# Retention plus two feed-forward layers: the second batch's state products on the other two array quadrants

## The chip, the cores and the metric

The kernel runs on one core of a Trainium2 chip. Its time is the device time of one execution in microseconds (us); given are the median of three runs and one execution that the hardware profiler recorded. The engines: TensorE (PE, with its weight loads as PEld), VectorE (DVE), ScalarE (ACT), GpSimd (POOL) and SyncE (SP), which here issues all DMAs.

## What is computed

Retention over 2 batches, 8 heads, 768 positions and head size 64, and then two feed-forward layers, all in float32:

```python
for t in range(S):
    state = gamma * state + einsum('bhd,bhe->bhde', k[:, :, t], v[:, :, t])
    y[:, :, t] = scale * einsum('bhd,bhde->bhe', q[:, :, t], state)
x = y.transpose(0, 2, 1, 3).reshape(B * S, H * D)      # 1536 x 512
h = x @ w1_in;  x = softplus(h) @ w1_out               # 512 -> 2048 -> 512
h = x @ w2_in;  out = silu(h) @ w2_out
```

## The kernel before

**Retention in chunks.** The 768 positions of each batch are cut into 6 chunks of 128, so there are 12 chunks, numbered n with the batch as n % 2: chunks 2 and 3 are the same positions of the two batches. Heads are taken in four pairs. For a chunk, `att_scores` (line 161) multiplies keys and queries of a head (64 rows of the array), `att_mask` (line 172) puts on the decay on DVE, and `att_within` (line 180) multiplies the result by the values: 128 rows, 64 columns, the even head j = 0 of a pair into PSUM partitions 0 to 63 and the odd head j = 1 into 64 to 127 of the tile `py`. `att_across` (line 196) adds what earlier chunks left: queries scaled by GpSimd (`qp`, line 125) times the state `past`, 64 rows and 64 columns of the array per head. Head j reads SBUF partitions of half j and writes PSUM partitions of half j, so of the four 64x64 quadrants only the two on the diagonal work. `att_state` (line 143) adds the chunk's keys (`kp`, scaled by GpSimd, line 132) times values to the state in PSUM, and `att_past` (line 158) copies that to SBUF on ACT.

**The split.** The feed-forward products run as three matmuls of a rounded high part and a low part. `att_split` (line 210) makes these of a chunk's output: `xhi` on ACT from `py` (line 219), `xlo` = `py` - `xhi` on DVE (line 220). Four chunks make a block of 512 tokens. `gemm1(i, half)` (line 316) reads `xhi` and `xlo` of a whole block: steps 0 to 2 read chunks 0 to 3, steps 3 to 5 chunks 4 to 7, steps 6 to 8 chunks 8 to 11. Step 0 alone goes by halves of 256 tokens, chunks 0 and 1 first.

**Weights.** They arrive as 64-bit numbers. A unit of them is converted by one ACT copy (`z`, line 267), six DVE instructions (lines 274, 275, 284, 287, 290, 292) and one ACT copy (`whi`, line 303).

**Order.** The order of each engine's work is the order of the program text, written out by hand (lines 452 to 576): chunk pair 2 and 3 stands in the main text (lines 497 to 519); pairs 4, 6, 8 and 10 go through `att_pair` (line 222), each behind a `gemm1` of 12 matmuls and the conversion of a weight unit. After pair 10 the rest is feed-forward steps alone.

Of the kernel before, what the change touches and what calls it, by code (L numbers as in the profile page):

```python
# [9 lines left out]
F32 = mybir.dt.float32  # L10
# [4 lines left out]
AF = mybir.ActivationFunctionType  # L15
# [3 lines left out]
P = 128  # L19
B, H, S, D = 2, 8, 768, 64  # L20
NCH = S // P
NPAIR = H // 2
DM = H * D
# [52 lines left out]
def retention_ffn2_kernel(  # L76
# [9 lines left out]
    nc = tc.nc  # L86
    const = ctx.enter_context(tc.tile_pool(name="const", bufs=1))
# [12 lines left out]

    mask = const.tile([P, 2, NPAIR, P], F32, name="mask")
    cs = const.tile([P, H * NCH], F32, name="cs")
    zero = const.tile([P, DM], F32, name="zero")

# [2 lines left out]
    a_t, qs_t, qp_t, kp_t, ps_t, sc_t, py_t, x_t = {}, {}, {}, {}, {}, {}, {}, {}  # L109
    state = ps.tile([P, B, NPAIR, D], F32, tag="st", bufs=1, name="state")  # L110
    past = const.tile([P, B, NPAIR, D], F32, name="past")
# [13 lines left out]
    def att_scale_q(n):  # L125
        qp = apool.tile([P, NPAIR, P], F32, tag="qp", name=f"qp{n}")
        qp_t[n] = qp
        nc.gpsimd.tensor_tensor(
            out=qp.rearrange("p a t -> p (a t)"), in0=a_t[n][:, 0, :], in1=qs_t[n // B], op=ALU.mult
        )  # L130
# [12 lines left out]
    def att_state(n):  # L143
        b, c = n % B, n // B
        a, kp = a_t[n], kp_t.pop(n)
        for p in range(NPAIR):
            for j in range(2):
                h = 2 * p + j
                nc.tensor.matmul(  # L149
                    state[j * D : (j + 1) * D, b, p, :],  # L150
                    lhsT=kp[:, h, :],
                    rhs=a[:, 2, h * D : (h + 1) * D],
                    start=n == p == 0,
                    stop=c == NCH - 2,
                    skip_group_check=True,
                )

    def att_past():
        nc.scalar.activation(out=past, in_=state, func=AF.Copy)

    def att_scores(n):
        a = a_t[n]
        pj = [
            psa.tile([P, NPAIR, P], F32, tag=f"acc{2 * (n % 2) + j}", name=f"sc{n}_{j}") for j in range(2)
        ]
        for p in range(NPAIR):
            for j in range(2):
                r, s = slice(j * D, (j + 1) * D), slice(p * P, (p + 1) * P)
                nc.tensor.matmul(pj[j][:, p, :], lhsT=a[r, 1, s], rhs=a[r, 0, s], start=True, stop=True)  # L169
        ps_t[n] = pj  # L170
# [9 lines left out]
    def att_within(n):  # L180
        a, sc = a_t[n], sc_t.pop(n)
        py = ps.tile([P, NPAIR, P], F32, tag="py", name=f"py{n}")
        py_t[n] = py
        for p in range(NPAIR):
            for j in range(2):
                h = 2 * p + j
                nc.tensor.matmul(  # L187
                    py[j * D : (j + 1) * D, p, :],
                    lhsT=a[:, 2, h * D : (h + 1) * D],
                    rhs=sc[j][:, p, :],  # L190
                    start=(p == 0),
                    stop=(n < B and p == NPAIR - 1),
                    skip_group_check=True,
                )

    def att_across(n):
        py, qp = py_t[n], qp_t.pop(n)
        for p in range(NPAIR):
            for j in range(2):
                r = slice(j * D, (j + 1) * D)  # L200
                nc.tensor.matmul(  # L201
                    py[r, p, :],
                    lhsT=past[r, n % B, p, :],
                    rhs=qp[r, p, :],
                    start=False,
                    stop=(p == NPAIR - 1),
                    skip_group_check=True,
                )

    def att_split(n):  # L210
        py = py_t.pop(n)
        blk, o = n // CPB, (n % CPB) * P
        if o == 0:
            x_t[0, blk] = (
                xpool.tile([P, NPAIR, BLK], F32R, tag="xhi", name=f"xhi{blk}"),
                xpool.tile([P, NPAIR, BLK], F32R, tag="xlo", name=f"xlo{blk}"),
            )
        hi, lo = (t[:, :, o : o + P] for t in x_t[0, blk])
        nc.scalar.activation(out=hi, in_=py, func=AF.Copy)
        nc.vector.tensor_tensor(out=lo, in0=py, in1=hi.bitcast(F32), op=ALU.subtract)  # L220

    def att_pair(n):

        more = n + B < NC
        for b in range(B):
            att_within(n + b)
        for b in range(B):
            att_across(n + b)
            att_split(n + b)
        if more:  # L230
            for b in range(B):
                att_scale_q(n + B + b)
            for b in range(B):
                att_scores(n + B + b)
            for b in range(B):
                att_state(n + b)
            att_past()
            for b in range(B):
                att_mask(n + B + b)
            if n + B < NC - B:  # L240
                for b in range(B):
                    att_scale_k(n + B + b)
# [209 lines left out]
    with tc.manual_schedule():  # L452
        att_load(0, 0, 2)
        nc.sync.dma_start(out=mask, in_=mask_d)
        att_load(1, 0, 2)
        att_load(0, 2, 3)
        att_load(1, 2, 3)
        nc.sync.dma_start(out=cs, in_=cs_d)
        att_load(0, 3, 4)
        att_load(1, 3, 4)  # L460
        att_load(2, 0, 2)
        att_load(3, 0, 2)
        qs_load(1)
        w_load(0)
        att_load(2, 2, 3)
        att_load(3, 2, 3)
        w_load(1)
        att_load(2, 3, 4)
        att_load(3, 3, 4)
        att_load(4, 0, 2)  # L470
        nc.scalar.preload_act_table_set("softplus")
        nc.vector.memset(zero, 0.0)
        warm = ps.tile([P, BLK], F32, tag="h", bufs=1, name="warm")
        for _ in range(WARM):
            nc.tensor.matmul(warm, lhsT=zero[:, :P], rhs=zero, start=True, stop=True)

        att_scores(0)
        att_mask(0)
        att_scores(1)
        att_mask(1)  # L480
        att_within(0)
        att_split(0)
        att_within(1)
        att_split(1)
        att_scale_k(0)
        att_scale_k(1)
        att_state(0)
        att_state(1)
        att_past()
        att_load(5, 0, 2)  # L490
        att_load(4, 2, 3)
        att_load(5, 2, 3)
        qs_load(2)
        w_load(2)
        att_load(4, 3, 4)
        att_load(5, 3, 4)
        att_scores(2)
        att_mask(2)
        att_scores(3)
        att_mask(3)  # L500
        att_scale_q(2)
        att_scale_q(3)
        w_exponent(0)
        convert(0)
        att_within(2)
        att_within(3)
        w_exponent(1)
        att_across(2)
        att_split(2)
        att_across(3)  # L510
        att_split(3)
        gemm1(0, 0)
        gemm1(0, 1)
        att_scale_k(2)
        att_scale_k(3)
        att_state(2)
        att_state(3)
        convert(1)
        act1(0)
        att_past()  # L520
        for lo in (0, 2):
            att_load(6, lo, lo + 2)
            att_load(7, lo, lo + 2)
        w_load(3)
        att_scale_q(4)
        att_scale_q(5)
        att_scores(4)
        att_mask(4)
        att_scores(5)
        att_mask(5)  # L530
        att_load(8)
        qs_load(3)
        att_scale_k(4)
        att_scale_k(5)
        first(1)
        act2(0)
        w_exponent(2)
        convert(2)
        act2(1)
        att_pair(4)  # L540
        att_load(9)
        qs_load(4)
        att_load(10, 0, 3)
        for i, n in ((2, 6), (3, 8), (4, 10)):
            u = units[i][0]
            w_exponent(u)
            first(i)
            convert(u)
            if i < NLEAD - 1:
                act2(i)  # L550
            att_pair(n)
            if n == 6:
                qs_load(5)
                att_load(11, 0, 3)
        second(0)
        act2(4)
        first(5)
        for u in units[5]:
            w_exponent(u)
            convert(u)  # L560
        second(1)
        act2(5)
        second(2)
        first(6)
        for u in units.get(6, ()):
            w_exponent(u)
            convert(u)
        second(3)
        act2(6)
        second(4)  # L570
        for i in range(NLEAD + 2, N):
            step(i)
        for m in range(4):
            gemm2(N - 2, (m,))
            gemm2(N - 1, (m,))
            evacuate(N - 1, (m,))
# [60 lines left out]
```

## Time and profile before

| what | us |
|---|---|
| median of 3 runs (578.09 to 579.44) | 578.32 |
| the profiled execution | 577.85 |
| its span, first to last instruction | 575.9 |
| PE busy in the span | 568.8 |
| DVE busy | 370.1 |
| ACT busy | 197.9 |
| POOL busy | 43.4 |

The profiled execution took 577.85 us, of which 575.9 us lie between its first and its last instruction; it is 0.47 us below the median. Retention and the first steps of the feed-forward lie in the first 64 us or so. In the chain of work that ended last PE has 96% of the span, but this is a figure of the whole span; what the change touches lies in the first eighth.

### The profile page before, as it was taken

The numbers are of one execution on the slowest core, as the hardware profiler recorded it, in microseconds if no ns is written. First come the engines' busy times: TensorE is split into PE (matmuls) and PEld (weight loads), VectorE is DVE, ScalarE is ACT, GpSimd is POOL, SyncE is SP. The second block draws the span as 40 slices with busy tenths as digits, with TensorE's granted clock in tenths as the row PEclk, the third lists the DMA queues.
The fourth block names the chain that finished last, engine by engine and source line by source line (L and its number), as shares of the span: only waits on it lengthen the run. The fifth ranks groups of instructions, "written<-read, shape, count | busy, mean of one in ns | idle before, by whom it ended". The sixth has DMA issues, their size and how long they took to land.

```text
span 575.9 us, 7532 instructions
## 1 busy us (share of the span) xinstructions
PE 568.8 (99%) x3026; PEld 470.2 (82%) x3026; DVE 370.1 (64%) x613; ACT 197.9 (34%) x363; POOL 43.4 (8%) x36
## 2 busy tenths in 40 slices
PE   8999999999999999999999999999999999999997
PEld 5888888888888888888888888888888888888885
DVE  3999458566854865785769863675566764783232
ACT  2343244423423423334336434343234233242120
POOL 1547000000000000000222210000000000000000
PEclk9999999999999999999999999999999999999999
DMA  8994122221211321221213211222113212100111
GB/s 298 399 410 159 36 75 78 69 73 38 99 48 36 110 73 38 73 77 70 74 36 110 74 49 61 73 73 75 36 40 107 74 36 74 49 25 0 74 73 74
DMA packets 15730, 51.10 MB, mean 89 GB/s; under 512 B 1872, under 2 KB 1872, under 8 KB 15440
## 3 DMA queue, kind: packets, MB, share of 16 engines
q1 hardware_dynamic: 15696, 50.63, 25.2%
q8 instruction: 24, 0.39, 0.3%
q14 instruction: 10, 0.08, 0.0%
HBM read 47.47 MB, written 3.15 MB: 88 GB/s over the span
## 4 chain that ended last, share of the span: by engine, by line
PE 96%; DMA 1%; DVE 1%; SPq 1%; POOL 0%; ACT 0%; issue 0%; DVEq 0%; POOLq 0%
PE acc L370 45%; PE h L331 45%; PE sc L169 2%; PE py L201 1%; PE py L187 1%; DMA att<-in_att 1%; PE state L149 1%; POOL kp L136 0%; SPq L123 0%; DVE scm L177 0%; DVE xlo L220 0%; DVE a L287 0%; DVE m L275 0%; DVE part L385 0%; ACT whi L303 0%
## 5 line engine op out<-in xcount | busy, mean ns | idle before, releaser
L347 ACT ACTIVATE ghi<-h 128x512 fp32r<-128x512 f32 x96 | 57.4, 598 | 334.0 <-PE h L331 322.7
L354 DVE TENSOR_TENSOR glo<-t,ghi 128x512 fp32r<-128x512 f32 x96 | 68.1, 714 | 40.4 <-ACT t L348 40.4
L385 DVE TENSOR_TENSOR part<-acc,part 128x512 f32<-128x512 f32 x84 | 57.4, 692 | 50.0 <-PE acc L370 50.0
L331 PE MATMUL h<-xhi,wlo 128*128 128x512 f32 (+1 forms) x196 | 76.0, 388 | 0.0
L331 PE MATMUL h<-xlo,whi 128*128 128x512 f32 (+1 forms) x196 | 75.6, 386 | 0.1
L331 PE MATMUL h<-xhi,whi 128*128 128x512 f32 (+1 forms) x196 | 75.4, 385 | 0.0
L370 PE MATMUL acc<-ghi,wlo 128*128 128x512 f32 x192 | 74.8, 390 | 0.0
L370 PE MATMUL acc<-ghi,whi 128*128 128x512 f32 x192 | 74.7, 389 | 0.0
L370 PE MATMUL acc<-glo,whi 128*128 128x512 f32 x192 | 74.7, 389 | 0.0
L331 PE MATMUL h<-yhi,wlo 128*128 128x512 f32 x192 | 74.7, 389 | 0.0
L331 PE MATMUL h<-ylo,whi 128*128 128x512 f32 x192 | 74.7, 389 | 0.0
L331 PE MATMUL h<-yhi,whi 128*128 128x512 f32 x192 | 74.7, 389 | 0.0
L370 PE MATMUL acc<-whi,glo 128*128 128x512 f32 x192 | 74.7, 389 | 0.0
L370 PE MATMUL acc<-wlo,ghi 128*128 128x512 f32 x192 | 74.7, 389 | 0.0
L370 PE MATMUL acc<-whi,ghi 128*128 128x512 f32 x192 | 74.7, 389 | 0.0
L284 DVE TENSOR_SCALAR z<-z 128x512 uint32<-128x512 uint32 x64 | 28.2, 441 | 71.2 <-ACT z L267 71.2
L348 ACT ACTIVATE t<-h 128x512 f32<-128x512 f32 x96 | 56.9, 593 | 0.0
L287 DVE SCALAR_TENSOR_TENSOR a<-raw,z 128x512 uint32<-128x512 uint32 x64 | 46.2, 722 | 2.2
L275 DVE SCALAR_TENSOR_TENSOR m<-raw,m 128x512 uint32<-128x512 uint32 x64 | 45.4, 710 | 2.2
L292 DVE SCALAR_TENSOR_TENSOR wlo<-m,z 128x512 fp32r<-128x512 int32 x64 | 45.0, 704 | 2.2
L303 ACT ACTIVATE whi<-a 128x512 fp32r<-128x512 f32 x64 | 40.5, 633 | 11.8 <-DVE a L287 11.8
L267 ACT ACTIVATE z<-raw 128x512 f32<-128x512 f32 x64 | 42.7, 668 | 1.6 <-DMA raw<-in_wts 1.6
(41 smaller groups left out, 682.7 us busy)
## 6 DMA issues: line engine op xcount, KB each, us to landing
raw<-in_wts SPq DMA_DIRECT2D x64, 512.0 KB, 3.3
att<-in_att SPq DMA_DIRECT2D x10, 512.0 KB, 7.4
att<-in_att SPq DMA_DIRECT2D x12, 256.0 KB, 7.1
out<-part SPq DMA_DIRECT2D x12, 256.0 KB, 2.1
att<-in_att SPq DMA_DIRECT2D x2, 1024.0 KB, 8.6
att<-in_att SPq DMA_DIRECT2D x2, 768.0 KB, 6.2
qs<-in_qs SPq DMA_DIRECT2D x5, 256.0 KB, 6.8
mask<-in_mask SPq DMA_DIRECT2D x1, 512.0 KB, 5.4
```

The costliest lines, as they stand in the source:

```text
L267: nc.scalar.activation(out=z, in_=raw_t[u][:, :, 1].bitcast(F32), func=AF.Copy, scale=2.0**-112)
L275: nc.vector.scalar_tensor_tensor(out=m, in0=raw[:, :, 1], scalar=23, in1=m, op0=ALU.logical_shift_left, op1=ALU.bitwise_or)
L284: nc.vector.tensor_scalar(out=z, in0=z, scalar1=3, scalar2=4, op0=ALU.logical_shift_left, op1=ALU.bitwise_or)
L287: nc.vector.scalar_tensor_tensor(out=a, in0=raw[:, :, 1], scalar=0x80000000, in1=z, op0=ALU.bitwise_and, op1=ALU.bitwise_or)
L292: nc.vector.scalar_tensor_tensor(out=lo, in0=m.bitcast(I32), scalar=2.0**-43, in1=z.bitcast(F32), op0=ALU.mult, op1=ALU.mult)
L303: nc.scalar.activation(out=hi, in_=a, func=AF.Copy)
L331: nc.tensor.matmul(ph[:, t], lhsT=w[:, s], rhs=x[:, kc, t], start=kc == o == j == 0, stop=kc == NPAIR - 1 and j == 2, skip_group_check=i == 0,
L347: nc.scalar.activation(out=ghi, in_=ph, func=f)
L348: nc.scalar.activation(out=t, in_=ph, func=f)
L354: nc.vector.tensor_tensor(out=glo, in0=t, in1=ghi.bitcast(F32), op=ALU.subtract)
L370: nc.tensor.matmul(acc_t[m], lhsT=lhsT, rhs=rhs, start=(first and j == 0), stop=(last and j == 2))
L385: nc.vector.tensor_tensor(out=part[:, m, :], in0=acc_t[m], in1=part[:, m, :], op=ALU.add)
```

## The change

Chunks of the second batch (odd n) keep the heads of a pair in exchanged halves of the PSUM tile: `half(n, j)` gives partitions of half j for even n and of the other half for odd n. `att_across` takes both chunks of a pair at once and goes through pair of heads, batch, head, so that four matmuls in a row are on the four 64x64 quadrants. `att_split` of an odd chunk first copies the two halves of `py` crosswise into an SBUF tile `turned` (two ACT instructions of 64 partitions by 512), and then makes `xhi` and `xlo` from `turned`. To make room, the tile of zeros for the first three matmuls is gone; `past` is set to zero and read in its place.

```diff
-    zero = const.tile([P, DM], F32, name="zero")
+    turned = const.tile([P, NPAIR, P], F32, name="turned")
@@ att_within
-                    py[j * D : (j + 1) * D, p, :],
+                    py[half(n, j), p, :],
+    def half(n, j):
+        j ^= n % B
+        return slice(j * D, (j + 1) * D)
+
     def att_across(n):
-        py, qp = py_t[n], qp_t.pop(n)
+        qp = [qp_t.pop(n + b) for b in range(B)]
         for p in range(NPAIR):
-            for j in range(2):
-                r = slice(j * D, (j + 1) * D)
-                nc.tensor.matmul(
-                    py[r, p, :],
-                    lhsT=past[r, n % B, p, :],
-                    rhs=qp[r, p, :],
+            for b in range(B):
+                for j in range(2):
+                    r = slice(j * D, (j + 1) * D)
+                    nc.tensor.matmul(
+                        py_t[n + b][half(n + b, j), p, :],
+                        lhsT=past[r, b, p, :],
+                        rhs=qp[b][r, p, :],
@@ att_split
+        if n % B:
+            for j in range(2):
+                nc.scalar.activation(out=turned[half(0, j)], in_=py[half(1, j)], func=AF.Copy)
+            py = turned
         nc.scalar.activation(out=hi, in_=py, func=AF.Copy)
         nc.vector.tensor_tensor(out=lo, in0=py, in1=hi.bitcast(F32), op=ALU.subtract)
@@ att_pair
+        att_across(n)
         for b in range(B):
-            att_across(n + b)
             att_split(n + b)
@@ main text
-        nc.vector.memset(zero, 0.0)
+        nc.vector.memset(past, 0.0)
+        zero = past.rearrange("r b p e -> r (b p e)")
...
         att_across(2)
         att_split(2)
-        att_across(3)
         att_split(3)
```

## Rows read from the trace of the kernel before

**Rows 1.** The page: span, and busy time of each engine with its share.
```profile
span 575.9 us, 7532 instructions
PE 568.8 (99%) x3026; PEld 470.2 (82%) x3026; DVE 370.1 (64%) x613; ACT 197.9 (34%) x363; POOL 43.4 (8%) x36
```
**Rows 2.** By stretch: us, busy us (PE, PEld, DVE, ACT, POOL), clock, DMA share, GB/s.
```profile
32.00:40.00 8.00, 8.00 (x114) 6.87 (x112) 7.83 (x15) 3.12 (x6) 0.74 (x1) 1.00 1.03 409
...
64.00:72.00 8.00, 8.00 (x37) 6.62 (x36) 2.91 (x5) 2.90 (x6) 0.00 (x0) 1.00 0.00 0
```
**Rows 3.** The chain that ended last, to 72 us: start, us, engine and line.
```profile
21.49 0.69 DVE xlo L220
...
22.22 1.57 PE h L331 x11
...
31.70 1.89 PE py L201 x32
...
35.58 1.08 PE state L149 x32
```
**Rows 4.** Timeline, TensorE: start, us, engine, line, operation, out<-in, count, [idle before <-releaser].
```profile
33.52 2.06 PE L169 MATMUL sc<-att 64*128 64x128 f32 x32
...
39.54 1.97 PE L187 MATMUL py<-scm,att 128*64 128x128 f32 x32
...
42.47 0.85 PEld L201 LDWEIGHTS py<-qp,past 64*64 64x64 f32 x16 [0.18 <-POOL qp L128]
...
46.84 0.19 PEld L331 LDWEIGHTS h<-xlo,whi 128*128 128x128 f32 x1
```
**Rows 5.** Timeline, ACT: the splits of chunks 1 to 5 and a copy of the state.
```profile
11.54 0.60 ACT L219 ACTIVATE xhi<-py 128x512 fp32r<-128x512 f32 x1 [0.69 <-PE py L187]
13.43 0.60 ACT L159 ACTIVATE past<-state 128x512 f32<-128x512 f32 x1 [1.29 <-PE state L149]
...
20.26 1.08 ACT L219 ACTIVATE xhi<-py 128x512 fp32r<-128x512 f32 x2
...
33.40 1.07 ACT L219 ACTIVATE xhi<-py 128x512 fp32r<-128x512 f32 x2
```
**Rows 6.** Timeline, DVE: masks of chunk 2, chunk 4's split to chunk 7's, line 287 later.
```profile
14.50 2.48 DVE L177 TENSOR_TENSOR scm<-sc,mask 128x512 f32<-128x512 f32 x4 [1.64 <-PE sc L169]
...
34.53 1.28 DVE L220 TENSOR_TENSOR xlo<-py,xhi 128x512 fp32r<-128x512 f32 x2
...
38.12 0.41 DVE L274 TENSOR_SCALAR m<-raw 128x512 uint32<-128x512 uint32 x1
...
39.18 0.42 DVE L284 TENSOR_SCALAR z<-z 128x512 uint32<-128x512 uint32 x1
39.63 1.65 DVE L287 SCALAR_TENSOR_TENSOR a<-raw,z 128x512 uint32<-128x512 uint32 x1
41.31 1.38 DVE L290 TENSOR_SCALAR z<-a 128x512 uint32<-128x512 uint32 x1
42.73 1.41 DVE L292 SCALAR_TENSOR_TENSOR wlo<-m,z 128x512 fp32r<-128x512 int32 x1
44.07 1.53 DVE L354 TENSOR_TENSOR glo<-t,ghi 128x512 fp32r<-128x512 f32 x1
45.52 1.27 DVE L220 TENSOR_TENSOR xlo<-py,xhi 128x512 fp32r<-128x512 f32 x2
...
59.97 0.69 DVE L287 SCALAR_TENSOR_TENSOR a<-raw,z 128x512 uint32<-128x512 uint32 x1
60.70 0.43 DVE L290 TENSOR_SCALAR z<-a 128x512 uint32<-128x512 uint32 x1
```
**Rows 7.** Timeline, POOL, from 39 us.
```profile
39.26 3.16 POOL L128 TENSOR_TENSOR qp<-att,qs 128x512 f32<-128x512 f32 x2 [8.50 <-DMA qs<-in_qs]
42.37 2.68 POOL L136 TENSOR_TENSOR kp<-att,cs 128x512 f32<-128x512 f32 x2
45.01 2.99 POOL L128 TENSOR_TENSOR qp<-att,qs 128x512 f32<-128x512 f32 x2
```

More of the change, by code (lines that the diff above doesn't have):

```diff
@@ L194, in att_within @@
                 )
+    def half(n, j):
+        j ^= n % B
+        return slice(j * D, (j + 1) * D)
     def att_across(n):
-        py, qp = py_t[n], qp_t.pop(n)
+        qp = [qp_t.pop(n + b) for b in range(B)]
         for p in range(NPAIR):
-            for j in range(2):
-                r = slice(j * D, (j + 1) * D)
-                nc.tensor.matmul(
-                    py[r, p, :],
-                    lhsT=past[r, n % B, p, :],
-                    rhs=qp[r, p, :],
[L205 to L208, printed above, removed]
+            for b in range(B):
[5 more added lines that the diff above has]
+                        rhs=qp[b][r, p, :],
+                        start=False,
+                        stop=(p == NPAIR - 1),
+                        skip_group_check=True,
+                    )
     def att_split(n):
```

## The prediction

> **What bounds the kernel now.** I read the page's busy times first: TensorE is busy for 99% of the span, VectorE for 64% and ScalarE for 34% [rows 1]. That invites a simple sum: the state products get shorter, so the kernel does. The shares are averages, though, so I read the table by stretch next, where the change is made. From 32 to 40 us VectorE is busy 7.83 of 8 us beside a full TensorE; from 64 us on it has 2.91 of 8 [rows 2]. So the retention stage has two engines at their limit, and only behind it does TensorE alone count. There a delay or a gain of TensorE goes into the end time one to one. Third, the chain of waits: it passes through the state products of line 201 at pair 4, but at pair 2 it goes through `xlo` on VectorE into `gemm1(0)` [rows 3]: there the split of chunk 3 is what TensorE waits for. Fourth, the timeline at 46.8 us: the second product of `gemm1(3)`, which reads `xlo` of chunks 4 to 7, starts its weight load at 46.84 [rows 4], 0.05 us after the two `xlo` of chunks 6 and 7, which run from 45.52 for 1.27 us [rows 6]. So VectorE's order of work has a second gate, and it is closed already.
>
> **State products on four quadrants.** Before, a pair of chunks takes 1.89 us in the chain for 32 records of line 201, two for each of 16 matmuls [rows 3]; two quadrants work at a time. What four would take no row shows. Not under the 1.08 us that the 32 records of line 149 need [rows 3]: they are two at a time as well, but half as long (64 columns), so this is a pace that TensorE is seen to take such instructions at. Not over 1.89 us: the records of line 187 bring two streams of 128 columns through every row of the array, those of line 169 two results to every column, in 1.97 and 2.06 us [rows 4], no slower than with the diagonal quadrants; four quadrants ask for both at once and for nothing else. Nor is a loss to be expected, since number and size of the matmuls stay. I take 1.08, because both halves of what is asked for are in the rows: a gain of 0.81 us for each of five pairs. That `att_within` writes an odd chunk's heads in exchanged halves changes nothing in number or order of the two tiles: 0.
>
> The Trainium skill speaks against it: "TensorEngine Tiling (Array Packing)", section Restrictions and Gotchas, says that different row tiles cannot access one PSUM bank at the same time. Two row tiles write one `py` tile here before and after, and the 1.89 us before are no longer than line 187's, which has no row tiles; so the trace does not bear the rule out for different partitions. By the rule the gain would be nothing, which is the second rival below.
>
> **The turn on ScalarE.** Two copies of 64 partitions and 512 elements are added for each odd chunk. No row has 64 partitions; the nearest are copies of `py` with 128: 0.60 us alone [rows 5], two behind each other 1.08, so 0.48 from start to start. As each partition has the same 512 elements, I take these, with nothing as the other end. `xhi` of the odd chunk now waits for both copies: it starts 0.48 + 0.48 + 0.60 = 1.56 us behind the even chunk's `xhi` and not 0.48, about 1.1 us later. Queued behind it on ScalarE are the state's copy and the weight copies, which keep their dates or gate VectorE as below. `xlo` of an odd chunk now reads SBUF twice instead of PSUM and SBUF; I take the same time, and price the other end below.
>
> Chunk 1: its `xhi` goes from 11.54 to 12.65, ends at 13.25, ahead of the state's copy at 13.43; its `xlo` ends by 14.0, ahead of the masks at 14.50 [rows 5, 6]. Cost 0, hidden by the wait for the next scores; if that cover of 0.2 to 0.5 us were gone, what overshoots would be added.
>
> Chunk 3: `xhi` of chunks 2 and 3 run from 20.26 for 1.08 us [rows 5]; now the second ends at 22.4, so `xlo` starts at 22.5 and not 21.49, and the matmuls released by it at 22.22 [rows 3] start at 23.2: **+1.0 us**. The shorter state products don't help here, since the chain doesn't pass through them: `gemm1(0)` waits for the weights and the split. Everything behind on TensorE and VectorE moves by 1.0.
>
> **Pair 4.** TensorE gets 0.81 back and is 0.2 late. VectorE does not: behind `xhi` of chunk 4, at 33.40 [rows 5], come the two copies, so `xlo` of chunk 5 is late by at least 33.40 + 1.08 + 1.1 = 35.6 against 35.13 (half of the two from 34.53 [rows 6]): 0.5 us, even if the lag of 1.0 were made up by then. If none of it is, 1.5. With 0.17 us of idle time in 8 [rows 2] there is little to make it up with, and a weight unit's copies, which wait for VectorE, stand ahead of the split on ScalarE; I take **1.3 us** at the masks of chunks 6 and 7.
>
> **What that lag runs into.** GpSimd waits for a DMA until 39.26 us and then works without a gap: two `qp`, two `kp`, two `qp` [rows 7], and two more `kp`. Beside it the VectorE instructions that read SBUF alone take turns with it: the last three of the weight unit and `glo` take 1.65, 1.38, 1.41 and 1.53 us [rows 6], while the same forms take 0.69 and 0.43 at 60 us, when GpSimd has nothing to do [rows 6]. That is 0.96, 0.95, 0.72 and 0.84 more, 0.87 in the mean. `xlo` at 45.52, which reads PSUM, keeps its time. The first three instructions of that unit, from 38.12 to 39.18 [rows 6], got through just ahead of GpSimd. Late by 1.3, the first would start at 39.42: all three fall behind GpSimd's first instruction, 3 x 0.87 = 2.6 us. GpSimd has eight instructions, enough to block seven. The transfer that starts it isn't moved: the DMA engines are at 1.03 of their share in this stretch [rows 2]. So `xlo` of chunk 7 is 1.3 + 2.6 = **3.9 us** late, and so is `gemm1(3)`. What TensorE won at pairs 4 and 6 goes into this wait. Pair 6 had little to win anyway: its second half waited for `qp` at 42.47 [rows 4], and the interleaved order needs both `qp` from its third matmul.
>
> The Trainium skill, "SBUF — State Buffer", section SBUF: two separate sides, calls the port pair that VectorE and GpSimd share an exclusive lock, taken by an instruction with two SBUF inputs too; the rows above agree. By it the new `xlo` of odd chunks would be blocked as well where GpSimd is at work.
>
> From the rows on `glo` that would be up to 0.87 more at chunk 7, which I leave to the range, as GpSimd is near its end by then.
>
> **Sum.** +3.9 at `gemm1(3)`; pairs 8 and 10 behind it give 2 x 0.81 = 1.6 back, and from 64 us on nothing else waits; `xlo` of chunk 11 has some us of slack. The exchange of the zero tile costs 0: a memset of the same size, and `past` is first overwritten at 13.43 [rows 5], long after the first matmuls. Net +2.3 us: the profiled execution of 577.85 us (575.9 of span and 1.95 around it) would take 580.15; the median of 578.32, 0.47 above it, **580.6 us**.
>
> **Rivals.** *Fewer fall behind* (0.20): the lag at 39 us is only 0.5; then one instruction (39.18 + 0.5) is blocked: 0.5 + 0.9 - 1.6 = -0.2, 578.1 us. For it: the lag depends on three waits that I bounded, not measured. *Quadrants don't overlap* (0.25): no four-way row exists; then no gain at any pair, +3.9 or a little more: 582.2 us or above. *No one falls behind* (0.08), the case that isn't slower: if the copies of 64 partitions are so short that VectorE's lag at 39.2 us is under 0.07 (39.26 - 39.18 is 0.08), `gemm1(3)` keeps its date and pairs 8 and 10 give 1.6: 576.7 us. Against it: even with no lag from pair 2 the chain of copies alone makes 0.5.
>
> **How the numbers follow.** The forecast has 0.47; with a lag of 1.0 to 1.5 and `xlo` blocked or not it covers about +1.4 to +3.2 us. About 0.3% of the time, 1.7 us (580.05), is what a measurement of this kernel can tell from no change. Slower: two thirds of the forecast and all but little of the second rival, 0.57. Faster: only the lower end of the last rival, 0.05. Same: 0.38. The range leaves out most of the last rival and the upper end of the second: 577.5 to 582.8.
>
> **What would show it.** Right: the 32 records of line 201 in about 1.1 us at each pair; `gemm1(0)` waiting for `xlo` until 23.2; the weight unit at 39 us with six or seven VectorE instructions of about 1.4 us instead of four; TensorE idle for some 3 to 4 us before the second product of `gemm1(3)`, released by `xlo`; no other new wait behind 50 us. Wrong: a weight unit that still starts before GpSimd; 32 records in 1.9 us; or a wait at the masks of pairs 8 and 10, which I take to be covered.

## The result and the profile after

The changed kernel takes 584.06 us in the median of 11 runs (582.42 to 584.66) against 578.31; the ratio is 1.0078 with a 95% interval of 1.0051 to 1.0106. It is slower, by 4.5 us by the ratio and 5.7 between the medians. The kernel before scatters more: three of its eleven runs took 581.0 to 585.2 us, and no trace of such a run was taken. The forecast had the sign and the wait in front of `gemm1(3)`, but at +2.3 us only half of the size or less, and the time lies 1.3 us above its range.

The profiled execution took 582.42 us, with a span of 580.3. Where the 4.4 us of span lie is quickly bounded. From the first matmul of `second(0)` to the end the two kernels take the same, 512.7 us: that matmul starts at 67.55 and not at 63.18. These are the rows, first of the kernel before, then of the changed one (timeline, TensorE: start, us, line, operation, out<-in):

```profile
63.18 0.50 PE L370 MATMUL acc<-ghi,wlo 128*128 128x512 f32 x1
```

```profile
67.55 0.50 PE L381 MATMUL acc<-ghi,wlo 128*128 128x512 f32 x1
```

So the reader can leave everything behind 68 us aside. The page of the changed kernel: span, and busy time by engine. ScalarE has 7.4 us more than in [rows 1], for the twelve copies; TensorE has 1.9 us less and yet the span is longer.

```profile
span 580.3 us, 7545 instructions
PE 566.9 (98%) x3026; PEld 467.4 (81%) x3026; DVE 370.0 (64%) x613; ACT 205.3 (35%) x375; POOL 43.0 (7%) x36
```

The table by stretch (columns as in [rows 2]) shows where: from 48 to 56 us TensorE is busy 5.14 of 8 us, VectorE 7.90, and the granted clock is 0.79 in the mean; 1.00 is 2.4 GHz. Inside that stretch, in this run, it is 1.00 while TensorE stands still, falls to 0.50, which is 1.2 GHz, at 51.5 us, 0.15 us after TensorE began again, and is back at 1.00 from 54.9 us on.

```profile
48.00:56.00 8.00, 5.14 (x18) 3.65 (x20) 7.90 (x13) 2.31 (x5) 4.21 (x3) 0.79 0.52 167
...
50.00:51.30 1.30, 0.00 (x0) 0.00 (x0) 1.30 (x3) 0.12 (x1) 1.30 (x2) 1.00 0.59 227
...
52.00:53.00 1.00, 1.00 (x4) 0.81 (x3) 1.00 (x2) 0.00 (x0) 0.21 (x1) 0.50 0.42 172
```

The chain that ended last (start, us, engine and line) answers [rows 3]: the state products, now line 208, take 1.03 us at pair 8 and not 1.89, so four quadrants do work at a time. But the chain reaches them only behind a part of `gemm1(3)` that takes 4.38 us for 11 matmuls.

```profile
51.36 4.38 PE h L342 x11
55.74 1.90 PE py L189 x32
57.64 1.03 PE py L208 x32
```

The timeline of TensorE in front of it. The first product waited for `xhi` and the second, whose weights were loaded at 46.84 before [rows 4], for `xlo`. From the third on one starts every 0.43 us, where 0.23 is normal:

```profile
49.13 0.51 PE L342 MATMUL h<-xhi,wlo 128*128 128x512 f32 x1 [1.36 <-ACT xhi L230]
51.36 0.69 PE L342 MATMUL h<-xlo,whi 128*128 128x512 f32 x1 [1.73 <-DVE xlo L231]
51.84 0.63 PE L342 MATMUL h<-xhi,whi 128*128 128x512 f32 x1
52.27 0.63 PE L342 MATMUL h<-xhi,wlo 128*128 128x512 f32 x1
...
55.67 1.09 PE L189 MATMUL py<-scm,att 128*64 128x128 f32 x16
```

In the kernel before, the second product of `gemm1(3)` and the first matmuls of pair 8 (timeline, TensorE):

```profile
46.90 0.45 PE L331 MATMUL h<-xlo,whi 128*128 128x512 f32 x1
...
49.58 1.97 PE L187 MATMUL py<-scm,att 128*64 128x128 f32 x32
```

VectorE from the split of chunk 3 on (timeline, the lines that answer [rows 6]; a weight unit is lines 285, 286, 295, 298, 301, 303):

```profile
23.22 0.69 DVE L231 TENSOR_TENSOR xlo<-turned,xhi 128x512 fp32r<-128x512 f32 x1 [1.19 <-ACT xhi L230]
...
26.08 1.53 DVE L301 TENSOR_SCALAR z<-a 128x512 uint32<-128x512 uint32 x1
27.65 1.64 DVE L303 SCALAR_TENSOR_TENSOR wlo<-m,z 128x512 fp32r<-128x512 int32 x1
...
38.38 0.69 DVE L231 TENSOR_TENSOR xlo<-turned,xhi 128x512 fp32r<-128x512 f32 x1 [0.68 <-ACT xhi L230]
...
41.38 1.30 DVE L285 TENSOR_SCALAR m<-raw 128x512 uint32<-128x512 uint32 x1
42.72 1.41 DVE L286 SCALAR_TENSOR_TENSOR m<-raw,m 128x512 uint32<-128x512 uint32 x1
44.05 1.26 DVE L295 TENSOR_SCALAR z<-z 128x512 uint32<-128x512 uint32 x1
45.35 0.69 DVE L298 SCALAR_TENSOR_TENSOR a<-raw,z 128x512 uint32<-128x512 uint32 x1
46.07 0.43 DVE L301 TENSOR_SCALAR z<-a 128x512 uint32<-128x512 uint32 x1
46.53 1.65 DVE L303 SCALAR_TENSOR_TENSOR wlo<-m,z 128x512 fp32r<-128x512 int32 x1
48.11 1.75 DVE L365 TENSOR_TENSOR glo<-t,ghi 128x512 fp32r<-128x512 f32 x1
...
50.38 0.92 DVE L231 TENSOR_TENSOR xlo<-turned,xhi 128x512 fp32r<-128x512 f32 x1
```

Here the lag grows: `xlo` of chunk 3 is 1.7 us later than before, that of chunk 5 (38.38 against about 35.13) 3.2 us, that of chunk 7 (50.38 against 46.12, the second of the two from 45.52) 4.3 us. Each holds 0.5 us by which this run lies behind already at 17 us, in the first loads; most profiled runs of the experiments, those made from the kernel before among them, lie 0.2 to 0.5 behind there, so this is hardly the change's. GpSimd (timeline) has its two `qp` at 26.05 just ahead of line 301, and a gap in front of its third pair, where it waits for a load:

```profile
26.05 2.69 POOL L130 TENSOR_TENSOR qp<-att,qs 128x512 f32<-128x512 f32 x2 [3.22 <-DMA qs<-in_qs]
...
39.87 2.53 POOL L130 TENSOR_TENSOR qp<-att,qs 128x512 f32<-128x512 f32 x2 [8.68 <-DMA qs<-in_qs]
...
46.24 3.07 POOL L130 TENSOR_TENSOR qp<-att,qs 128x512 f32<-128x512 f32 x2 [1.21 <-DMA qs<-in_qs]
```

In the kernel before, the instructions that are now lines 301 and 303 were through, or all but through, when GpSimd started (VectorE, then GpSimd):

```profile
24.65 0.43 DVE L290 TENSOR_SCALAR z<-a 128x512 uint32<-128x512 uint32 x1
25.11 0.69 DVE L292 SCALAR_TENSOR_TENSOR wlo<-m,z 128x512 fp32r<-128x512 int32 x1
25.77 2.53 POOL L128 TENSOR_TENSOR qp<-att,qs 128x512 f32<-128x512 f32 x2 [3.22 <-DMA qs<-in_qs]
```

How that delay reaches chunk 5 shows in the chain that ended last of the changed kernel: `gemm1(1)` waits for the late `wlo`, ScalarE's copy `z` of the next weight unit stands behind two instructions that wait for `gemm1(1)`, and VectorE waits for `z`.

```profile
27.65 1.65 DVE wlo L303
...
29.43 3.02 PE h L342 x12
...
33.56 0.57 ACT z L278
...
34.16 0.44 DVE z L295
```

And ScalarE at chunks 2 and 3, against [rows 5]:

```profile
20.73 0.58 ACT L230 ACTIVATE xhi<-py 128x512 fp32r<-128x512 f32 x1
21.33 1.20 ACT L228 ACTIVATE turned<-py 64x512 f32<-64x512 f32 x2
22.56 0.63 ACT L230 ACTIVATE xhi<-turned 128x512 fp32r<-128x512 f32 x1
```

The first copy starts when `xhi` has ended and the second when the first has ended, 0.60 us from start to start, not 0.48 as two copies of 128 partitions.

### The profile page after: what moved, and what is told of

Same layout as the page of the kernel before. It is cut to its first block, busy times and chain, and to the rows that moved or that the text cites. A ratio compares the mean times of both kernels' runs of the same rounds, so it can differ in the third digit from the quotient of the medians.

```text
span 580.3 us, 7545 instructions
## 1 busy us (share of the span) xinstructions
PE 566.9 (98%) x3026; PEld 467.4 (81%) x3026; DVE 370.0 (64%) x613; ACT 205.3 (35%) x375; POOL 43.0 (7%) x36
## 4 chain that ended last, share of the span: by engine, by line
PE 91%; DVE 4%; ACT 1%; DMA 1%; issue 1%; SPq 0%; POOL 0%; DVEq 0%; POOLq 0%
PE acc L381 45%; PE h L342 44%; DMA att<-in_att 1%; DVE scm L179 1%; PE py L189 1%; DVE wlo L303 1%; PE sc L171 1%; DVE a L298 0%; DVE m L286 0%; ACT turned L228 0%; ACT xhi L230 0%; DVE z L295 0%; PE py L208 0%; POOL kp L138 0%; DVE m L285 0%
## 5 line engine op out<-in xcount | busy, mean ns | idle before, releaser
L365 DVE TENSOR_TENSOR glo<-t,ghi 128x512 fp32r<-128x512 f32 x96 | 66.5, 697 | 40.4 <-ACT t L359 40.4
L303 DVE SCALAR_TENSOR_TENSOR wlo<-m,z 128x512 fp32r<-128x512 int32 x64 | 46.2, 722 | 2.2
L342 PEld LDWEIGHTS h<-xhi,wlo 128*128 128x128 f32 x196 | 37.2, 190 | 12.0 <-ACT xhi L230 2.4
L342 PEld LDWEIGHTS h<-xlo,whi 128*128 128x128 f32 x196 | 37.1, 190 | 10.0 <-DVE xlo L231 2.6
```

Source lines behind the costliest of these rows:

```text
L303: nc.vector.scalar_tensor_tensor(out=lo, in0=m.bitcast(I32), scalar=2.0**-43, in1=z.bitcast(F32), op0=ALU.mult, op1=ALU.mult)
L342: nc.tensor.matmul(ph[:, t], lhsT=w[:, s], rhs=x[:, kc, t], start=kc == o == j == 0, stop=kc == NPAIR - 1 and j == 2, skip_group_check=i == 0,
L365: nc.vector.tensor_tensor(out=glo, in0=t, in1=ghi.bitcast(F32), op=ALU.subtract)
```

## The experiments

**Theory.** The copies of the turn make VectorE late; late, its weight conversions fall behind GpSimd's start, take at least twice as long beside it and keep the next splits waiting; `gemm1(3)` waits for the split of chunk 7, and after the wait TensorE runs at half clock. **Rivals:** the four-quadrant order itself costs time; or the turn's latency alone does it, and GpSimd has no part.

**One part at a time.** First the turn without the four quadrants: each chunk's products on their own again.

```diff
     def att_across(n):
+        for b in range(B):
+            att_across_one(n + b)
+
+    def att_across_one(n):
+        qp = qp_t.pop(n)
         for p in range(NPAIR):
-            for b in range(B):
-                for j in range(2):
+            for j in range(2):
...
```

> The changed kernel with the state products two quadrants at a time again, one chunk after the other; the exchange and the turn on ScalarE stay. If the turn alone makes the loss (my theory): the wait of gemm1(3) for xlo stays, some 4.5 us later than in the kernel before, its clock falls likewise, and pairs 8 and 10 no longer give back 0.87 us each, so 1.7 us above the changed kernel: 584.5 to 586. If the four-quadrant order itself costs the time (rival): back near the kernel before, 578 to 580.

Measured: 584.69 us, ratio 1.0079 (1.0044 to 1.0115). The loss is all there without the four quadrants, and the quadrants are not its cause. Their gain is smaller than I had put it here, 0.6 us between the medians. Part of the reason is in the trace: with the exchange, and one chunk after the other, the 32 records take 1.59 us in the timeline, against 1.96 in the kernel before and 1.10 in the order of the changed kernel. The second chunk's products seem to begin beside the first's. Then the quadrants without the turn:

```diff
-        if n % B:
-            for j in range(2):
-                nc.scalar.activation(out=turned[half(0, j)], in_=py[half(1, j)], func=AF.Copy)
-            py = turned
```

> The changed kernel without the two copies: odd chunks are split straight from PSUM, so their heads stay exchanged (the turn of the halves is left out). If the turn alone makes the loss: line 208's 32 records still take 1.03 us, gemm1(3) waits for xlo about when it did before, 46.8 us, and only pairs 8 and 10 gain: 1.7 us below the kernel before, 576.6. If every pair's gain reached the end it would be 574. If the four-quadrant order itself costs time: 582 or above.

Measured: median 577.34 us (576.31 to 584.19), ratio 0.9995 (0.9955 to 1.0035), which alone decides nothing. The trace, of one of the faster runs (576.62), does: the two `xlo` of chunks 6 and 7 keep their time,

```profile
45.84 1.28 DVE L226 TENSOR_TENSOR xlo<-py,xhi 128x512 fp32r<-128x512 f32 x2
```

and `second(0)` starts at 61.76, 1.4 us earlier than in the kernel before although the run lies 0.5 us later at 17 us: about the 1.7 us that pairs 8 and 10 win. What pairs 4 and 6 win is lost in front of `gemm1(3)`, as the prediction had it.

**How early.** A constant, 4 in one kernel and 8 in the other, sets the first chunk that is exchanged, turned and put on four quadrants:

```diff
+TURN_FROM = 4
     def half(n, j):
-        j ^= n % B
+        j ^= n % B if n >= TURN_FROM else 0
```

> Exchange, turn and four quadrants from chunk 4 on; chunks 1 to 3 as in the kernel before. If pair 2's turn starts the loss and later ones only add to it: VectorE is on time at 26 us, is about 0.7 us late at the masks of pair 6 and has one or two more instructions in GpSimd's way; gemm1(3) 2 to 3 us late, less by 1.7 from pairs 8 and 10: 578.5 to 581. If pair 2 alone makes the loss: 576.6. If pair 2 has no part in it: 583 as the changed kernel.

> Exchange, turn and four quadrants for chunks 8 to 11 alone. By my theory nothing before 50 us moves, VectorE has room for the later xlo behind gemm1(3), and both pairs give 0.87 us: 576.6, ratio 0.997. If the turn costs wherever it stands: 578 or above.

Measured: from 4 on 580.03 us, ratio 1.0017 (0.9991 to 1.0044); from 8 on 576.98, ratio 0.9959 (0.9936 to 0.9983). Between the medians, leaving chunks 1 and 3 (and pair 2's products) as before saves 4.0 us, leaving chunks 5 and 7 too another 3.1, and the turn of the last two costs nothing that shows: behind 50 us the quadrants' gain comes out, and this version beats both kernels, by 0.4%. The first median mixes unlike runs: five of the ten took 578.7 to 579.6 us at a mean granted clock of 1.00, five 580.5 to 583.6 at 0.994 to 0.997. The runs from 8 on scatter from 576.1 to 580.8. Their profiled run (VectorE's timeline, 577.66 us) shows what can delay them: VectorE is 0.2 us later than in the kernel before, and the third instruction of the unit (`z`, here line 315) has lost its place ahead of GpSimd, 1.51 us where [rows 6] has 0.42.

```profile
38.77 0.69 DVE L306 SCALAR_TENSOR_TENSOR m<-raw,m 128x512 uint32<-128x512 uint32 x1
39.38 1.51 DVE L315 TENSOR_SCALAR z<-z 128x512 uint32<-128x512 uint32 x1
```

**GpSimd's part.** Its scaling is left out of both kernels; the matmuls read queries and keys as loaded.

```diff
     def att_scale_q(n):
...
+        qp_t[n] = a_t[n][:, 0, :].rearrange("p (a t) -> p a t", a=NPAIR)
     def att_scale_k(n):
...
+        kp_t[n] = a_t[n][:, 3, :].rearrange("p (h d) -> p h d", h=H)
```

> The kernel before with GpSimd's scaling of queries and keys left out: the matmuls read queries and keys as loaded. It is the base for the next run. The last three VectorE instructions of the weight unit at 40 us and glo should take 0.69, 0.43, 0.69 and 0.68 us. TensorE bounds the stage then: 577 to 578.4, little different from the kernel before.

> The changed kernel with the same scaling on GpSimd left out. If the loss is VectorE in GpSimd's way, brought there by the turn (my theory): no VectorE instruction over 0.8 us before 60 us, xlo of chunk 7 at most 1 us late at gemm1(3), and the run is 1 to 2.5 us faster than the kernel before without GpSimd, 575 to 577. If the turn's own latency makes the loss (rival): gemm1(3) still 3 us or more late, 580 or above.

Measured: 579.62 us (ratio 1.0004, 0.9980 to 1.0028) and 578.08 (0.9969, 0.9940 to 0.9998). Without GpSimd the changed kernel is not slower but 1.5 us faster between the medians, as far as runs tell that overlap (577.8 to 580.4 and 575.1 to 579.1). Both times miss their ranges, by 1.2 and 1.1 us: in both profiled runs TensorE waits 2.6 us for loads between 15 and 19 us, which the two kernels with GpSimd don't, and whether that makes the miss was not tried. The edit also takes away the matmuls' waits for GpSimd's results, so by itself it doesn't show that VectorE's waiting is all of GpSimd's part; the runs with VectorE's order mended, below, keep GpSimd. The unit at 42 us runs in its own time (VectorE, changed kernel without GpSimd):

```profile
43.60 0.69 DVE L286 SCALAR_TENSOR_TENSOR a<-raw,z 128x512 uint32<-128x512 uint32 x1
44.33 0.43 DVE L289 TENSOR_SCALAR z<-a 128x512 uint32<-128x512 uint32 x1
44.79 0.69 DVE L291 SCALAR_TENSOR_TENSOR wlo<-m,z 128x512 fp32r<-128x512 int32 x1
...
47.57 0.69 DVE L219 TENSOR_TENSOR xlo<-turned,xhi 128x512 fp32r<-128x512 f32 x1 [0.88 <-ACT xhi L218]
```

Another part of the expectation missed as well: `xlo` of chunk 7 is 2.2 us later than in its base (45.32), not 1 at most. What is left is the turn's own latency, and a half clock from 17.5 to 20.9 us in this run, which its base has not; the two were not told apart. Together they cost 1.0 us at the first matmul of pair 8 (51.59 against 50.59), and the quadrants behind make up for it.

**The step of the prediction by itself.** In the kernel before, `xlo` of chunk 5 is made three times, which puts 1.2 us in front of the unit at 38 us and nothing else:

```diff
-        nc.vector.tensor_tensor(out=lo, in0=py, in1=hi.bitcast(F32), op=ALU.subtract)
+        for _ in range(3 if n == 5 else 1):
+            nc.vector.tensor_tensor(out=lo, in0=py, in1=hi.bitcast(F32), op=ALU.subtract)
```

> The kernel before with xlo of chunk 5 made three times over on VectorE, 1.2 us more ahead of the masks and the weight unit at 38 us. By the step of the prediction (three more instructions behind GpSimd, 0.87 each): xlo of chunk 7 3.8 us late, at 49.9 instead of 46.1, gemm1(3) too, and with the clock as in the changed kernel up to 1.4 more: 582 to 583.6. If GpSimd adds nothing: 1.2 us, 579.5.

Measured: 584.78 us, ratio 1.0086 (1.0059 to 1.0114), more than expected: 1.2 us of work on an engine that is busy 64% of the span cost 5 us or so. All seven VectorE instructions are blocked, and the two `xlo` start at 50.03 and not at 45.52:

```profile
39.72 1.52 DVE L275 TENSOR_SCALAR m<-raw 128x512 uint32<-128x512 uint32 x1
...
44.14 1.41 DVE L288 SCALAR_TENSOR_TENSOR a<-raw,z 128x512 uint32<-128x512 uint32 x1
...
50.03 1.28 DVE L221 TENSOR_TENSOR xlo<-py,xhi 128x512 fp32r<-128x512 f32 x2
```

That is 4.5 us for 1.2 (0.3 of it from the start of the run); the rest of the loss is the clock, at 0.5 from 49.1 to 55.9 us.

**The clock.** The wait of the changed kernel is filled with 12 matmuls into the tile that `gemm1(3)` overwrites.

```diff
+        if i == 3 and half == 0:
+            for kc in range(3 * NPAIR):
+                nc.tensor.matmul(ph, lhsT=w_t[2, 0][0][:, :P], rhs=x_t[0, 0][0][:, kc % NPAIR, :], start=True, stop=True)
```

> The changed kernel with 12 more matmuls of 512 columns on TensorE ahead of gemm1(3), into the same PSUM tile, which gemm1(3) then overwrites: some 2.8 us of work in a wait of 3.6 us. If the fall of the granted clock to 0.5 from 51.5 to 54.9 us comes from the idle time ahead of it: the clock stays 1.0, the 11 matmuls take 2.7 us instead of 4.4 and the run is 1.4 to 1.7 us below the changed kernel, 582.4 against 584.1. If the fall has another cause: no gain, the clock row stays at 0.79 for 48 to 56 us.

Measured: 581.64 us, ratio 1.0046 (1.0023 to 1.0069). The wait for `xlo` is still there, TensorE has 1.5 us without work in it, and the clock stays at 1.00 in the profiled run:

```profile
48.00:56.00 8.00, 6.46 (x49) 4.98 (x49) 7.93 (x12) 2.63 (x5) 3.06 (x3) 1.00 0.38 144
```

From the second product to the first matmul of pair 8 it takes 2.8 us here (51.66 to 54.42) and not 4.3. So useless work makes the kernel 2.4 us faster between the medians; the half clock is a cost of the idle time, over and above the wait. The filling doesn't keep the clock up in every run: the four longest of the twelve (582.3 to 583.2 us) have a mean clock of 0.995 to 0.997.

**The copies.** The same two copies without the exchange of halves:

```diff
-                nc.scalar.activation(out=turned[half(0, j)], in_=py[half(1, j)], func=AF.Copy)
+                nc.scalar.activation(out=turned[half(1, j)], in_=py[half(1, j)], func=AF.Copy)
```

> The changed kernel with the two copies of py made into the same half they come from, so the exchange isn't undone. In the changed kernel two copies take 1.20 us, start to start 0.60, and the first waits for the xhi ahead of it. If that comes from moving data to other partitions: now start to start 0.48, two in 1.08, xhi of chunk 3 about 0.25 us earlier. If it comes from 64 partitions instead of 128: still 1.20.

Still 1.20 us for two, start to start 0.60, so moving the data to other partitions isn't what keeps the copies apart. Whether it is the 64 partitions or the change of the starting partition from one to the next was not tried.

```profile
21.11 1.20 ACT L228 ACTIVATE turned<-py 64x512 f32<-64x512 f32 x2
```

As this edit changes no time on ScalarE, its one run (583.51 us) is a second trace of what the changed kernel does, and it is like most of that kernel's runs: its mean granted clock is 0.994, as in eight of the eleven, where the profiled run has 0.997. Six VectorE instructions are blocked in it and not five, `xlo` of chunk 7 starts at 51.04, and the clock is 0.50 from about 49.6 to 56.4 us. It fell while TensorE still had nothing to do (table by stretch):

```profile
50.00:51.00 1.00, 0.00 (x0) 0.00 (x0) 1.00 (x2) 0.00 (x0) 1.00 (x1) 0.50 0.97 387
```

**Mending VectorE's order.** If the splits are late because conversions stand in front, it should help to put the conversions behind: those of steps 2 and 3 make weights for the second products (`w1_out`), which no one reads before `second(0)`, at 63.18 us in the kernel before. Three kernels have this edit: the changed one, the one with `TURN_FROM = 8`, and the kernel before.

```diff
-            convert(u)
+            if i == 4:
+                convert(u)
             if i < NLEAD - 1:
                 act2(i)
             att_pair(n)
+            if i < 4:
+                convert(u)
```

> The changed kernel, all turns kept; only the conversions of the weight units at steps 2 and 3 (second-layer weights, not needed before 63 us) stand behind the pair's split and masks on VectorE. If the loss is VectorE's splits queued behind conversions that GpSimd blocks: xlo of chunk 7 starts by 46 us instead of 50.4, gemm1(3) doesn't wait for more than 1 us, the clock stays 1.0, and the gain of the quadrants comes out: about 2 us below the kernel before, 576.2, and 7 below the changed kernel. If the turn's latency itself makes the loss: 582 or above.

> Turn and four quadrants for chunks 8 to 11 alone, and the same two conversions later. Both help apart: the conversions give about 0.3 us at gemm1(3), the quadrants 1.7 at pairs 8 and 10: 576.2, ratio 0.996. If the first turns are harmless once VectorE's order is mended, no better than the changed kernel with late conversions.

> The kernel before with the same two conversions later: the base for the two runs above. By my theory gemm1(3) already waits a little for VectorE: 0.3 us faster, 578.0, hardly to be told from no change.

All three missed: 584.93, 583.18 and 584.91 us, ratios 1.0095, 1.0061 and 1.0085. `xlo` of chunk 7 did come early (44.4 us in the kernel before, 46.0 in the changed one), but 10 us later all three wait for a load. A conversion also issues the next weight load, which waits on SyncE's queue until VectorE has read the buffer; moved back, it stood in front of chunk 11's loads (in the kernel before with this edit it is issued at 50.88 us and not at 41.36, and chunk 11's load behind it at 51.79 and not at 46.23). TensorE in the kernel before with this edit:

```profile
58.49 1.87 PE L169 MATMUL sc<-att 64*128 64x128 f32 x14 [3.89 <-DMA att<-in_att]
```

I had read who waits for the conversion, but not what its DMA stands in front of. The same three, with chunk 11's loads issued ahead of the conversion:

```diff
             att_pair(n)
-            if i < 4:
-                convert(u)
             if n == 6:
                 qs_load(5)
                 att_load(11, 0, 3)
+            if i < 4:
+                convert(u)
```

> The kernel before with the two conversions behind the pair's split and masks as in the last runs, and the loads of chunk 11 issued ahead of the conversion, so that SyncE doesn't hold them back behind a weight load that waits for VectorE (which made TensorE wait 3.9 us for them at 58.5 us). Base for the next two: gemm1(3) no longer waits for VectorE, 0.3 us faster than the kernel before, 578.0.

> The changed kernel, all turns and four quadrants kept, with the same two moves. If the loss is VectorE's splits queued behind conversions that GpSimd blocks: no wait over 1 us at gemm1(3), clock 1.0 from 48 to 56 us, and the quadrants' gain comes out: 576 to 577, 7 us below the changed kernel. If the turn's own latency makes it: 582 or above.

> Turn and four quadrants for chunks 8 to 11 alone, with the same two moves: 576.2, ratio 0.996, as turn_from_8 or up to 0.5 us better, without its scatter, since no VectorE instruction ahead of gemm1(3) stands just in front of GpSimd's start any more.

Measured: 578.35 us (ratio 0.9986, 0.9967 to 1.0005), 576.79 (0.9957, 0.9934 to 0.9981) and 576.55 (0.9956, 0.9936 to 0.9977). With VectorE's order mended the changed kernel, all its turns kept, is 7.3 us faster than without; the kernel before gains nothing in the median by the same two moves. That settles the rival: the turn's latency alone doesn't make the loss. VectorE in it: the two splits stand in front, at 44.75 and 46.63, and TensorE is busy all the time from 48 to 56 us at full clock.

```profile
44.75 0.69 DVE L231 TENSOR_TENSOR xlo<-py,xhi 128x512 fp32r<-128x512 f32 x1 [1.02 <-ACT xhi L230]
46.63 1.03 DVE L231 TENSOR_TENSOR xlo<-turned,xhi 128x512 fp32r<-128x512 f32 x1 [1.19 <-ACT xhi L230]
```

```profile
48.00:56.00 8.00, 8.00 (x129) 6.80 (x130) 6.78 (x12) 3.75 (x7) 4.00 (x4) 1.00 0.48 165
```

The early turns are harmless then but bring nothing either: with the turn from chunk 8 on alone the time is the same within the intervals, and the runs lie closest, 576.1 to 577.0. These two versions beat both kernels, by 0.4%. The two moves seem to help the kernel before as well, at the upper end of its times: of 29 runs without them, taken beside these, seven lie above 580 us, five of those with a mean clock of 0.996 or 0.997; of the 12 with them none lies above 579.5. As none of those seven was traced, that VectorE's order makes them is not shown.

## Why the prediction was half right

The step that failed is the sum: behind the 3.9 us at `gemm1(3)` it has only the 1.6 us that pairs 8 and 10 give back, and no term for what the wait does to TensorE's clock. In the profiled run the late start measured 4.5 us (0.5 of it the run's own), what comes back 1.7, and the half clock behind the wait 1.6 us that stood at nothing. By its own steps:

- **State products: right.** Taken as 1.08 us, measured 1.03, a gain of 0.86, which comes out at pairs 8 and 10 alone, as forecast. The bound was not strict, though: 1.03 lies just under the 1.08 that I had as the least. The rule of the Trainium skill ("TensorEngine Tiling (Array Packing)", Restrictions and Gotchas) that row tiles cannot access one bank at a time did not hold for tiles on different partitions.
- **The price of the two copies: too low.** I took 0.48 from start to start from copies of 128 partitions [rows 5]. They take 0.60, and the first waits for the `xhi` ahead of it: `xhi` of chunk 3 starts 1.83 us behind that of chunk 2, not 1.56.
- **Pair 4, the lag of 1.3 us: the step that was mis-sized first.** It was 3.2, 2.8 without the run's later start, beyond the 1.5 that I took as its upper bound. I bounded it by the chain of copies and by pair 2's lag, and asked at 39 us only what falls behind GpSimd. GpSimd starts another stretch at 25.77 in the kernel before. The 1.0 us that I had for pair 2 would have put line 292 behind it (25.11 + 1.0) and line 290 just ahead (24.65 + 1.0); in the profiled run, 1.4 us late there with the run's own 0.5, both fell behind, line 301 by 0.03 us. They took 1.53 and 1.64 us instead of 0.43 and 0.69, 2.0 us more. VectorE makes up 1.6 of this, as two later instructions, blocked before (`glo` 1.45 and `m` 1.26), now run free. It loses as much again by the wait for `z`, which is late by way of `gemm1(1)` (0.8), and by the copies (0.7). The same question had to be asked at every start of GpSimd.
- **Three more instructions behind GpSimd, 2.6 us: too high for what the lag had become.** In the profiled run VectorE came so late that GpSimd ran out of work in between, since a load that waits for chunk 4's buffer was late too: five instructions were blocked, not seven. The lag grew by 1.0 us. With a lag of 1.2 us and nothing else changed (the kernel with `xlo` three times) all seven were blocked, and `xlo` came 4.2 us late where the step, with the 1.2, gives 3.8. The new `xlo` of chunk 7, for which I had left up to 0.87 us to the range, took 0.92 instead of 0.69.
- **`gemm1(3)` 3.9 us late: right in sum, by luck.** Two errors stand against each other, the lag too small and what falls behind GpSimd too large. `xlo` of chunk 7 was 4.3 us late, 3.8 without the run's later start.
- **The clock: left out.** I had no term for what an idle TensorE does to the work behind it. From the second product of `gemm1(3)` to the first matmul of pair 8 it is 4.3 us (51.36 to 55.67) and was 2.7 (46.90 to 49.58): 1.6 us. So the span's sum is 4.5 for the later second product, 1.6 for the clock, less 1.7 at pairs 8 and 10: 4.4 us. The filled kernel shows that the idle time makes it: there the loss is 3.3 us between the medians, not 5.7.
- **The median.** The account above is of the profiled run, the fastest of the eleven; the median of 584.06 lies 1.6 us above it. The run with straight copies, 1.1 us above it, shows where most of that can lie: 0.65 us in the second product, which starts at 52.01, and 0.45 in a half clock that lasts until pair 8 starts at 56.76. That the other runs are like it is not shown; their mean clocks (0.994 in eight, 0.997 in three) speak for it.

The rivals: the quadrants overlap, and more fell behind GpSimd, not fewer. That the wait costs twice, once as a wait and once as half clock behind it, would have been worth a rival.

## What to carry to other kernels

Find the engine that is at its limit in the stretch that is changed, and ask of every start of a shared resource, not of one, which instructions a small delay moves behind it: 1.2 us on VectorE cost 5 here. Work that isn't urgent (weights needed 20 us later) belongs behind the split that TensorE waits for, and whoever moves it moves its DMA on the queue too. Shorter matmuls were worth something here only behind the last wait that another engine sets: the same four-quadrant products bring 1.4 to 1.7 us with VectorE's order mended or from chunk 8 on, and with the turn a loss of 4.5 otherwise.

## What the runs showed of the hardware

- Four 64x64 quadrants work at a time on float32 products with two streams of 128 columns through each row half: 32 records in 1.03 us instead of 1.89.
- Two ScalarE copies of 64 partitions by 512 start 0.60 us apart, two of 128 partitions 0.48, whether or not they exchange halves.
- Beside GpSimd, VectorE's subtraction with one input in PSUM kept its 0.68 us (the kernel with quadrants alone, two from 45.84 in 1.28); with both inputs in SBUF it took 0.92 in the changed kernel and 1.03 in that with VectorE's order mended, 0.69 without GpSimd.
- After one matmul in 3.6 us the granted clock was 0.50 for 3.4 us in the profiled run, from just behind TensorE's new start; with straight copies it fell while TensorE was still idle and was 0.50 for 6.8 us. With 1.5 us of idle time in the same place, in the filled kernel's profiled run, it did not fall.
